# Turning the token-mixing weight with DMAs instead of TensorE

## The chip, the cores and the metric

The kernel runs on one core of one Trainium2 chip. The metric is the device time of one execution in microseconds (us); a run's time is given as the median of several executions. All inputs and the output lie in DRAM (HBM) at the start and the end. Everything else that is shown here comes from one profiled execution: the engines TensorE (PE, with its weight loads as PEld), VectorE (DVE), ScalarE (ACT), GpSimd (POOL) and SyncE (SP), and the DMA queues. Times "at 39.6" are microseconds from the start of that execution's span.

## The reference, cut to what matters

Two blocks follow one another. The first is a block-sorted attention: four batches, eight heads, 768 tokens, head dimension 64; eight blocks of 96 tokens are mixed by an 8 x 8 matrix that five Sinkhorn rounds have normalised, and attention runs inside each block. The second is an MLP with residual on the 768 x 512 activation of each batch:

```python
def _moe_ref(x, alpha1, beta1, w_tok, alpha2, beta2, w_ch1, w_ch2, lam):
    a1 = alpha1 * x + beta1
    tok = np.einsum('ts,bsd->btd', w_tok, a1)
    u = x + lam * tok
    a2 = alpha2 * u + beta2
    ch = np.maximum(a2 @ w_ch1, 0.0) @ w_ch2
    return (u + lam * ch).astype(np.float32)
```

`w_tok` is 768 x 768 and mixes tokens. TensorE contracts over the partitions of both its operands, so the sum over `s` needs `w_tok` with `s` on partitions, that is, its transpose. DRAM holds it with `t` on rows.

## The kernel before

The work is cut by batch `b` (0 to 3). Each engine gets its instructions in the order in which the program text issues them (the schedule is written out by hand, with no planner), and waits inside that order for the data it needs.

**Loads.** GpSimd's queue issues the loads that convert float32 to a 16-bit type on the way: `rawk`, `qn`, `raw0`/`rawv` for k, q and v, then (L143 to L145) six row tiles `wt16[n]`, each 128 rows of `w_tok` as 128 x 768 bf16, taken from the rotating tile name `hT`, which has ten buffers and is used for the hidden activations later. After `load_q(1)` and `load_k(1)` it issues `W1` (L735) and `W2` (L737). GpSimd also runs arithmetic in the same queue, so a DMA issue that waits holds up the arithmetic behind it. A GpSimd load waits until the load eight places before it on that queue has landed: the four `W2` issues at L737 wait for the two halves of `qn` and the two of `rawk` of batch 1. SyncE's queue issues the plain DMAs: vectors at the start, `a1lB`, `b1lB` and `lamB` (L718 to L720), then nothing until `v_relay(1)` (L412, L418), and the results later.

**The weight's turn.** `w_tok_block(ks, eng, pool)` (L288) turns one column block: six TensorE transposes, one for each row tile, into one PSUM bank, and one eviction by VectorE or ScalarE (`copy`, L147 to L151) to `w_tokT[:, ks, :]`. Six calls stand between the attention steps of batch 0 (L764 to L775), two evicted by VectorE and four by ScalarE. `w_tokT[p, ks, t]` is `w_tok[t, ks * 128 + p]`.

**Batch 0's way to the MLP.** `soft(0, p, g)` (L484) is two groups of small matmuls into a bank of the pool `psA`, which has two buffers, and one exponential on ScalarE (L502). `value(0, p)` (L522) is 24 matmuls into a `psA` bank (L516), a reciprocal (L528) and a product (L529) on VectorE, which writes its columns of `x16[0]`. The order at the end is `soft(0, 3, 0)`, `soft(0, 3, 1)`, and then `value` for p = 2, 1, 0, 3. `token_mix(0, 0)` (L583) needs all of `x16[0]`: six matmuls with `w_tokT` as the stationary operand (L589); then, only once, `row_sums` (L299, 36 matmuls at L303), which sums each row of `w_tok`; `row_part` (L575) makes of it the bias tile `rb[:, kt]`, on VectorE and ScalarE for the first two and on GpSimd (L579) for the other four. For each `kt` GpSimd adds `x + rb` (L597), VectorE adds the mixed part (L601, L602), ScalarE rounds the sum to bf16 (L603). `u_turn` (L614) turns it back for the hidden layer.

**The steady part.** `hidden` (L635) and `result` (L672) are the two dense layers; `weave` mixes the steps of the next batch's attention into them by fixed costs, so the order on each engine is fixed there too. The hidden activations take over the `hT` buffers: with six of the ten used by `wt16`, the fifth pair of the first `hidden` is the first to reuse one of those six. `w_tokT` serves all four batches.

Of the kernel before, what the change touches and what calls it, by code (L numbers as in the profile page):

```python
# [11 lines left out]
BF = mybir.dt.bfloat16  # L12
# [7 lines left out]
def kernel(  # L20
# [18 lines left out]
    B, H, S, D = q.shape  # L39
# [4 lines left out]
    NT = S // 128  # L44
# [12 lines left out]
    psM = ctx.enter_context(tc.tile_pool(name="psM", bufs=3, space=bass.MemoryType.PSUM))  # L57
# [4 lines left out]
    def wt(shape, dtype, name):  # L62
        return wts.tile(shape, dtype, name=name, tag=name)
# [4 lines left out]
    def tmp(shape, dtype, name, bufs):  # L68
        return work.tile(shape, dtype, name=name, tag=name, bufs=bufs)
# [4 lines left out]
    def bank(pool, dtype=FT):  # L74
        n = 512 if dtype is FT else 1024
        tag = "psM" if pool is psM else "psX"
        return pool.tile([128, n], dtype, name=tag, tag=tag)

    V, A, PE, G, SP = nc.vector, nc.scalar, nc.tensor, nc.gpsimd, nc.sync
# [23 lines left out]
    w_tokT = wt([128, NT, S], BF, "w_tokT")  # L103
# [39 lines left out]
    wt16 = [tmp([128, S], BF, "hT", 10) for _ in range(NT)]  # L143
# [3 lines left out]
    def copy(eng, dst, src):  # L147
        if eng is A:
            A.copy(dst, src)
        else:  # L150
            eng.tensor_copy(dst, src)  # L151

    def v_first_layout(part, quarter, eng):
        n = D // 16
        d0 = (part * 4 + quarter) * n
        dst = v0T[:, 0:BLK * D].rearrange("r (d t) -> r d t", t=BLK)
        src = raw0[0:64].rearrange("r (t d) -> r d t", d=D)
        copy(eng, dst[:, d0:d0 + n], src[:, d0:d0 + n])
# [22 lines left out]
    identbf = wt([128, 128], BF, "identbf")  # L181
# [88 lines left out]
    def big_p(b):  # L270
# [13 lines left out]
            pq[:].unsqueeze(1).to_broadcast([128, 2 * H, NB]),  # L284
            m16[:].unsqueeze(2).to_broadcast([128, 2 * H, NB]), ALU.mult,
        )

    def w_tok_block(ks, eng, pool):  # L288
        ps = bank(pool, BF)
        for tt in range(NT):  # L290
            PE.transpose(
                ps[:, tt * 128:(tt + 1) * 128], wt16[tt][:, ks * 128:(ks + 1) * 128], identbf[:]
            )
        copy(eng, w_tokT[:, ks, :], ps[:, 0:S])

    rowsum = wt([128, NT], FT, "rowsum")
    rb = wt([128, NT, C], FT, "rb")
# [27 lines left out]
    def q_pair(b, p, pool, eng):  # L325
        ps = bank(pool, F16)
        q_turn(b, p, ps)
        q_copy(b, p, ps, eng)
# [58 lines left out]
    def v_first(g, eng, pool):  # L387
        ps = bank(pool)
        for dd in range(8):
            d0 = (g * 8 + dd) * BLK  # L390
            m = 128 if dd < 7 else BLK
            PE.matmul(
                ps[0:m, dd * 64:(dd + 1) * 64], v0T[:, d0:d0 + m],
                PB[0][0:64, 0].rearrange("r l p i -> r l (p i)"), start=True, stop=True,
            )
        copy(
            eng, vS[0][:, :, g * 8:(g + 1) * 8],
            ps[0:BLK].rearrange("p (d c) -> p c d", c=64),
        )
# [84 lines left out]
    def soft(b, p, g):  # L484
        ps = bankA()
        for i in range(4):
            c = (g * 4 + i) * BLK
            for hl in range(2):
                r = slice(hl * 64, hl * 64 + 64)
                PE.matmul(  # L490
                    ps[:, hl, i * BLK:(i + 1) * BLK], kT[r, p * S + c:p * S + c + 128],
                    qT[b % 2][p][r, c:c + BLK], start=True, stop=False, skip_group_check=True,
                )
            for hl in range(2):
                r = slice(hl * 64, hl * 64 + 64)
                n = p * NB + g * 4 + i
                PE.matmul(  # L497
                    ps[:, hl, i * BLK:(i + 1) * BLK],
                    nmask[r, n:n + 1].to_broadcast([64, 128]), tp_of[p][r, :],
                    start=False, stop=True, skip_group_check=True,  # L500
                )
        A.activation(  # L502
            exps(b, p)[:, :, g * 4:(g + 1) * 4, 0:BLK],
            ps[0:BLK, :, 0:4 * BLK].rearrange("p l (i t) -> p l i t", t=BLK),
            AF.Exp, scale=scale,
        )
# [15 lines left out]
    def value(b, p):  # L522
        ps = bankA()
        for hl in range(2):
            products(b, p, hl, ps[:, hl])
        xg = ps[:, :, 0:NT * VP].rearrange("p l (s e) -> p l s e", e=VP)
        recip = tmp([128, 2, NT], FT, "recip", 2)
        V.reciprocal(recip[:], xg[:, :, :, D])  # L528
        V.tensor_tensor(  # L529
            x16[b % 2][:].rearrange("p s (l h d) -> p l s h d", l=2, d=D)[:, :, :, p],  # L530
            xg[:, :, :, 0:D],
            recip[:].unsqueeze(3).to_broadcast([128, 2, NT, D]), ALU.mult,
        )
# [184 lines left out]
    SP.dma_start(a1lB[:], vecs[0].partition_broadcast(128))  # L718
    SP.dma_start(b1lB[:], vecs[1].partition_broadcast(128))
    SP.dma_start(lamB[:], moe_lam.partition_broadcast(128))  # L720
    v_first_layout(0, 0, A)
    q_pair(0, 2, psM, A)
    v_first_layout(0, 1, A)
# [37 lines left out]
    soft(0, 1, 0)  # L761
    turn_first(3, 3)
    soft(0, 1, 1)
    w_tok_block(3, V, psM)  # L764
    v_first(6, V, psM)
    soft(0, 3, 0)
    soft(0, 3, 1)
    w_tok_block(0, V, psM)
    w_tok_block(5, A, psM)
    value(0, 2)  # L770
    w_tok_block(2, A, psM)
    value(0, 1)
    w_tok_block(1, A, psM)
    value(0, 0)
    w_tok_block(4, A, psM)  # L775
    value(0, 3)
    first = ahead(1)
    next(first)
# [18 lines left out]
    for b in range(B):  # L797
        n = b + 1
# [61 lines left out]
```

## Time and profile before

| | |
|---|---|
| time before, median of 3 | 297.47 us (297.2 to 297.64) |
| the profiled execution's own time | 297.77 us |
| its span, first to last instruction | 295.9 us |
| around the span | 1.87 us |
| mean granted TensorE clock | 0.983 |
| busy: PE, PEld, DVE, ACT, POOL | 278.2, 166.4, 170.2, 143.3, 71.9 us |
| chain that ended last, by engine | PE 75%, DVE 9%, POOL 5%, DMA 4%, ACT 4% |
| the turn of `w_tok`: PE L291, DVE L151, ACT L149 | 36 of 219 ns, 2 of 557 ns, 4 of 799 ns |
| DMA moved | 27.09 MB, mean 92 GB/s |

The span is the stretch in which the profiled core executed instructions; the time of that execution is longer by what lies before and after it. Busy times are sums over overlapping pipelined instructions, so a busy engine isn't necessarily the limit. The chain that ended last is followed back from the last instruction: at each step either to what released that instruction or to the one before it on its engine, so its shares say where a microsecond less would have been a microsecond less at the end, until another chain takes over. GB/s and KB count bytes at the destination of a DMA; a load that converts float32 to 16 bits reads twice as many.

### The profile page before, as it was taken

Reading aid. Unit: us, or ns where it says so; the run is one execution under the profiler, and the core shown is the slowest. Engines: PE = TensorE matmul, PEld = TensorE weight load, DVE = VectorE, ACT = ScalarE, POOL = GpSimd, SP = SyncE. Lnnn points to the kernel's source line nnn. Section 1 sums busy time; section 2 is a strip of 40 time slices with the busy share of each in tenths; the row PEclk is TensorE's granted clock in tenths of the full one; section 3 lists DMA queues with packets and bytes.
Section 4 is the critical chain, followed back from the end, with each engine's and each line's share of the span. In section 5 each row is a group of like instructions: output and inputs, shape, how many; then the busy total and the mean of one; then the engine's idle time right before and its main releaser. Section 6 shows DMA issues by size and latency. Waiting matters only on the chain.

```text
span 295.9 us, 7069 instructions
## 1 busy us (share of the span) xinstructions
PE 278.2 (94%) x3059; PEld 166.4 (56%) x3078; DVE 170.2 (58%) x315; ACT 143.3 (48%) x244; POOL 71.9 (24%) x86
## 2 busy tenths in 40 slices
PE   8968997799999999999999999999999999899994
PEld 6647854365556555565566455565566445545643
DVE  7887756885262669594452679592444684123224
ACT  3285857665436446664246455664344126811500
POOL 8399549910000532200000810000000900000000
PEclk9985999999999999999999999999999999999999
DMA  6997999999610039990110049100110010002012
GB/s 115 210 225 156 186 212 229 215 216 214 85 52 24 0 127 113 198 205 3 38 71 2 1 134 126 64 0 2 63 48 1 2 71 35 0 2 81 25 38 72
DMA packets 32135, 27.09 MB, mean 92 GB/s; under 512 B 19724, under 2 KB 26920, under 8 KB 32040
## 3 DMA queue, kind: packets, MB, share of 16 engines
q0 software_dynamic: 8976, 14.81, 28.4%
q1 hardware_dynamic: 23128, 11.82, 18.2%
q8 instruction: 24, 0.39, 0.5%
q14 instruction: 7, 0.06, 0.1%
HBM read 32.79 MB, written 8.65 MB: 140 GB/s over the span
## 4 chain that ended last, share of the span: by engine, by line
PE 75%; DVE 9%; POOL 5%; DMA 4%; ACT 4%; issue 1%; DVEq 0%; POOLq 0%
PE psM L635 28%; PE psM L672 23%; PE psM L589 7%; DMA u<-in_v_dram 4%; PE psA L516 3%; PE psA L490 2%; DVE kT L151 2%; PE psA L430 2%; PE psA L497 2%; DVE u L602 2%; POOL rb L579 2%; ACT a2T L625 2%; POOL u L597 2%; DVE x L529 1%; DVE mx L435 1%
## 5 line engine op out<-in xcount | busy, mean ns | idle before, releaser
L635 PE MATMUL psM<-a2T,W 128*128 128x384 bf16 x512 | 90.8, 326 | 0.9 <-ACT a2T L625 0.7
L672 PE MATMUL psM<-W,hT 128*128 128x512 bf16 x349 | 83.9, 379 | 1.6 <-issue 1.0
L645 ACT ACTIVATE hT<-psM 128x384 bf16<-128x384 f32 x96 | 46.5, 491 | 50.4 <-PE psM L635 49.1
L635 PEld LDWEIGHTS <-W 128*128 128x128 bf16 x512 | 47.8, 98 | 32.5 <-issue 2.3
L597 POOL TENSOR_TENSOR u<-x,rb 128x512 f32<-128x512 f16 x24 | 28.5, 1214 | 142.6 <-DVE x L529 140.7
L672 PEld LDWEIGHTS <-hT 128*128 128x128 bf16 x368 | 34.2, 98 | 37.2
L681 DVE TENSOR_TENSOR tmix<-psM,lamB 128x512 f32<-128x512 f32 x23 | 15.9, 690 | 39.4 <-PE psM L672 39.3
L643 DVE TENSOR_SCALAR hT<-psM 128x384 bf16<-128x384 f32 x32 | 17.7, 553 | 31.6 <-PE psM L635 27.2
L589 PE MATMUL psM<-x,w_tokT 128*128 128x512 f16 x144 | 34.7, 379 | 0.6 <-DVE x L529 0.6
L502 ACT ACTIVATE ET<-psA 96x768 f16<-96x768 f32 x28 | 21.1, 803 | 28.0 <-PE psA L497 28.0
L435 DVE TENSOR_REDUCE mx<-psA 96x8 f32<-96x768 f32 x30 | 27.3, 948 | 3.9 <-PE psA L430 3.7
L603 ACT CAST u<-u 128x512 bf16<-128x512 f32 x24 | 14.8, 618 | 21.9 <-DVE u L602 21.8
L602 DVE TENSOR_TENSOR u<-u,tmix 128x512 f32<-128x512 f32 x24 | 20.3, 846 | 6.5 <-POOL u L597 4.5
L589 PEld LDWEIGHTS <-w_tokT 128*128 128x128 bf16 x144 | 13.4, 98 | 15.3 <-DVE x L529 1.1
L601 DVE TENSOR_TENSOR tmix<-psM,a1lB 128x512 f32<-128x512 f32 x24 | 16.4, 683 | 3.1 <-PE psM L589 3.0
L625 ACT ACTIVATE a2T<-psM,cols 128x384 bf16<-128x384 bf16 x24 | 16.1, 670 | 3.4 <-PE psM L619 3.4
L682 DVE TENSOR_TENSOR u<-u,tmix 128x512 f32<-128x512 f32 x23 | 16.9, 734 | 1.5
L529 DVE TENSOR_TENSOR x<-psA,recip 128x768 f16<-128x768 f32 x16 | 15.3, 957 | 0.6
L490 PEld LDWEIGHTS <-kT 64*128 64x128 f16 x256 | 12.3, 98 | 5.2 <-issue 5.1
L490 PE MATMUL psA<-qT,kT 64*128 64x96 f16 x256 | 15.1, 212 | 0.2 <-ACT ET L502 0.2
L497 PE MATMUL psA<-tp,nmask 64*128 64x96 bf16 x256 | 15.0, 211 | 0.0
L528 DVE RECIPROCAL recip<-psA 128x12 f32<-128x12 f32 x16 | 3.7, 229 | 19.1 <-PE psA L516 19.1
(121 smaller groups left out, 295.1 us busy)
## 6 DMA issues: line engine op xcount, KB each, us to landing
out_dram<-u SPq DMA_DIRECT2D x23, 256.0 KB
W<-in_moe_w_ch_dram POOLq DMA_DIRECT2D x8, 512.0 KB, 20.2
rawk<-in_k_dram POOLq DMA_DIRECT2D x8, 384.0 KB, 7.6
qn<-in_q_dram POOLq DMA_DIRECT2D x8, 384.0 KB, 9.1
rawv<-in_v_dram POOLq DMA_DIRECT2D x6, 384.0 KB, 13.6
vscr<-rawv SPq DMA_DIRECT2D x3, 768.0 KB
vS<-vscr SPq DMA_DIRECT2D x8, 192.0 KB
hT<-in_moe_w_tok_dram POOLq DMA_DIRECT2D x6, 192.0 KB, 13.4
```

The costliest lines, as they stand in the source:

```text
L435: V.tensor_reduce(mx[b % 2][:, :, c:c + 4], ps[0:BLK, :, 0:4 * BLK].rearrange("p l (i t) -> p l i t", t=BLK), AXX, ALU.max,)
L490: PE.matmul(ps[:, hl, i * BLK:(i + 1) * BLK], kT[r, p * S + c:p * S + c + 128], qT[b % 2][p][r, c:c + BLK], start=True, stop=False, skip_g ...
L497: PE.matmul(ps[:, hl, i * BLK:(i + 1) * BLK], nmask[r, n:n + 1].to_broadcast([64, 128]), tp_of[p][r, :], start=False, stop=True, skip_grou ...
L502: A.activation(exps(b, p)[:, :, g * 4:(g + 1) * 4, 0:BLK], ps[0:BLK, :, 0:4 * BLK].rearrange("p l (i t) -> p l i t", t=BLK), AF.Exp, scale ...
L529: V.tensor_tensor(x16[b % 2][:].rearrange("p s (l h d) -> p l s h d", l=2, d=D)[:, :, :, p], xg[:, :, :, 0:D], recip[:].unsqueeze(3).to_br ...
L589: PE.matmul(ps[:], w_tokT[:, ks, kt * 128:(kt + 1) * 128], x[:, ks, :], start=(ks == 0), stop=(ks == NT - 1),)
L597: G.tensor_tensor(ub[:, kt], x[:, kt], rb[:, kt], ALU.add)
L602: V.tensor_tensor(ub[:, kt], ub[:, kt], t[:], ALU.add)
L625: A.activation(t[:], ps[:, 0:TOK], AF.Identity, bias=cols2[:, 1, ci:ci + 1], scale=cols2[:, 0, ci:ci + 1])
L635: PE.matmul(ps[:, 0:TOK], W1[:, ci, m * 128:(m + 1) * 128], a2T_of[b, half, ci][:], start=(ci == 0), stop=(ci == CT - 1),)
L645: A.activation(t, ps[:, 0:TOK], AF.Relu)
L672: PE.matmul(ps[:], hT_of[m][:, kk * 128:(kk + 1) * 128], W2[:, m, :], start=(m == 0), stop=(m == HT - 1),)
```

## The change

The function `w_tok_block` and its six calls go. Behind the issue of `lamB` SyncE issues six transposing DMAs, one for each row tile, from `wt16[n]` in SBUF to its place in `w_tokT`, all six column blocks at once: 128 x 768 in, 128 x 6 x 128 out. Each starts when its row tile has landed. `token_mix(0, kt)` reads the columns that the DMA of row tile `kt` wrote; `row_sums` reads all. Nothing else changes.

```diff
-    def w_tok_block(ks, eng, pool):
-        ps = bank(pool, BF)
-        for tt in range(NT):
-            PE.transpose(
-                ps[:, tt * 128:(tt + 1) * 128], wt16[tt][:, ks * 128:(ks + 1) * 128], identbf[:]
-            )
-        copy(eng, w_tokT[:, ks, :], ps[:, 0:S])
-
...
     SP.dma_start(lamB[:], moe_lam.partition_broadcast(128))
+    for n in range(NT):
+        SP.dma_start_transpose(w_tokT[:, :, n * 128:(n + 1) * 128], wt16[n][:])
     v_first_layout(0, 0, A)
...
     soft(0, 1, 1)
-    w_tok_block(3, V, psM)
     v_first(6, V, psM)
     soft(0, 3, 0)
     soft(0, 3, 1)
-    w_tok_block(0, V, psM)
-    w_tok_block(5, A, psM)
     value(0, 2)
-    w_tok_block(2, A, psM)
     value(0, 1)
-    w_tok_block(1, A, psM)
     value(0, 0)
-    w_tok_block(4, A, psM)
     value(0, 3)
```

## Prediction

> **What bounds the kernel now.** I read four views of the profile of before. The first is the chain of work that ended last, between 28 and 60 us, since the change lies in that stretch (start, length, what):
>
> ```profile
> 31.38 1.42 ACT ET L502 x2
> ...
> 33.36 0.78 PE psM L291 x12
> 34.13 0.76 PE psA L516 x24
> ...
> 34.91 0.24 DVE recip L528
> ...
> 38.62 0.97 DVE x L529
> ...
> 39.64 1.47 PE psM L589 x6
> 41.11 0.89 PE psM L303 x36
> ...
> 42.86 1.16 POOL u L597
> 44.02 2.08 POOL rb L579
> ```
>
> Of the 36 turns (L291) only twelve are on the chain, 0.78 us. Then four value steps follow at VectorE's pace, 34.91 to 39.59, and the other turns and their evictions lie beside them. From 42.86 to 52.6 GpSimd sets the pace (L597 and L579 in turn); from 58.8 on the chain is TensorE's dense layers to the end. So a gain ahead of 39.6 reaches the end if GpSimd and the DMAs let it.
>
> The second view is the order of time on ScalarE and GpSimd (start, length, what, idle time before and its releaser):
>
> ```profile
> 32.78 1.50 ACT L502 ACTIVATE u<-psA 96x768 f16<-96x768 f32 x2
> ...
> 36.98 0.74 POOL L737 DMA_DIRECT2D W<-in_moe_w_ch_dram  x1 [0.93 <-DMA rawk<-in_k_dram]
> 40.14 0.74 POOL L737 DMA_DIRECT2D W<-in_moe_w_ch_dram  x1 [2.42 <-DMA rawk<-in_k_dram]
> 42.86 1.16 POOL L597 TENSOR_TENSOR u<-x,rb 128x512 f32<-128x512 f16 x1 [1.98 <-DVE rb L579]
> ```
>
> GpSimd's last W2 issue waits for the second half of rawk to land, at 40.1, and ends at 40.88; its next instruction is the first link of GpSimd's stretch of the chain, 1.98 us later. This is the thinnest cover that the change touches.
>
> The third view is busy time by stage, of which the last three columns count: granted TensorE clock, DMA share, GB/s.
>
> ```profile
> 16.00:18.00 2.00, 0.86 (x28) 0.55 (x24) 1.56 (x3) 1.52 (x3) 1.68 (x3) 1.00 1.16 210
> 20.00:22.00 2.00, 0.95 (x16) 0.56 (x13) 0.97 (x3) 1.51 (x3) 2.00 (x4) 0.50 1.09 256
> 26.00:28.00 2.00, 2.00 (x48) 1.92 (x47) 1.48 (x4) 1.48 (x3) 1.94 (x3) 0.50 0.56 107
> 28.00:30.00 2.00, 2.00 (x47) 1.69 (x46) 1.31 (x4) 1.42 (x2) 2.00 (x4) 0.56 0.44 26
> 30.00:32.00 2.00, 2.00 (x59) 1.65 (x54) 1.87 (x7) 1.90 (x4) 2.00 (x5) 1.00 1.15 174
> 36.00:38.00 2.00, 2.00 (x55) 1.82 (x53) 1.93 (x5) 1.36 (x3) 0.79 (x2) 1.00 1.02 204
> ```
>
> The DMA engines are full at some 210 GB/s except for one pocket. At 107, 26 and 174 GB/s the rows from 26 to 32 moved 614 KB, where 210 would have moved 1260: 646 KB, or 3.1 us of full DMA work, is free there. The fourth view, of what one tile's instructions wait for, gives the landing of the row tiles: 12.1 to 13.8 us after their issues at 5.0 to 10.1, so the first lands near 18.4 and the last between 22.2 and 23.9.
>
> **What the change removes.** Behind the exponentials TensorE does twelve turns and then value(0, 2). Without them value(0, 2) waits for the next thing, its psA bank. The pool has two, and the free one is that of soft(0, 3, 0), whose exponential is the first of the two that begin at 32.78 with 1.50 us, so it ends at 33.53. Add the 0.06 us between the end of an exponential and TensorE's next start (32.78 to 32.84). The 24 matmuls take 0.91 from their first start (33.97 to 34.88 in the order of time on TensorE): 33.59 + 0.91 = 34.50, reciprocal at 34.53 in place of 34.91. **Gain 0.38 us**, not 0.78. After it VectorE is full (0.23 + 0.96 with a small overlap for each value), so nothing more comes.
>
> The other 24 turns and the evictions are worth nothing: ScalarE's four, 3.2 us, end ahead of a copy of rawv that waits 0.81 us for TensorE, and VectorE's second ends at 34.40, ahead of a reciprocal that waits for TensorE until 34.91. The first lies under ScalarE's exponentials, which set soft(0, 3, ·). Six banks of psM go unused; no step on the chain waits for one.
>
> **What it adds.** Six issues on SyncE, free from 18.64 (end of lamB's issue) until 45.24. An issue of vS, the SyncE issue with the most small runs, holds the queue for 1.35 us (median of ten): 8.1 us for six, over well ahead of 45.24, where v_relay(1) stands behind them. The added waits: TensorE's L589 at 39.26 for the first DMA, row_sums at 40.7 for the other five, and all of TensorE stands behind either; the fifth hidden pair, at about 62 us, for the first DMA's reading.
>
> How long the data take, no row shows; nothing here transposes in a DMA. They are 1.18 MB in 4608 runs of 256 bytes. From below: plain copies with long runs flow at 354 GB/s (50 to 51 us, where vscr<-rawv goes out of SBUF): 3.4 us. From above: runs of 128 bytes, alone on the DMA engines (vS, 112 to 117 us), flow at 92 GB/s: 12.8 us. If the number of runs counts, 256 bytes go at twice that: 6.4 us. Below nothing is excluded, as DMA work is added. The source lies in SBUF with rows of 1536 bytes as in the first row, the destination runs are nearer to the second; I take 4.5 us, between 3.4 and 6.4 and nearer to the first because its source is SBUF too; this is a choice. The Trainium skill, DMA: Bandwidth & Descriptors, section Latency and other measured facts, gives 261 GB/s for transposing DMAs with a non-contiguous middle dimension; the sum by it would also be 4.5 us. No run here shows it.
>
> The DMAs start between 18.6 and 24 beside full queues and end in the pocket, near 30, ten us ahead of need. Of 4.5 us, 3.1 fit into the pocket; 1.4 push the later loads back. What that meets: rawk's second half, and with it GpSimd's L597, has 1.98 - 0.38 = **1.6 us of cover**; W1 lands at the latest near 31.9 + 18.7 = 50.6 and is needed at 57.0; vS, last of the full stretch, has until value(1, 0) at 80.0, and the DMA share falls to 0.17 after 78. So 1.4 is just hidden, and the cover is thin: each microsecond of DMA work above 4.7 us costs a microsecond.
>
> **Sum.** -0.38 + 0 = -0.4 us. The profiled execution, 297.77 us (span 295.9 and 1.87 around it), goes to 297.4; it lay 0.30 above the median, so I apply the same difference to the median: 297.47 - 0.38 = **297.1 us**.
>
> **The rivals.**
>
> Loads pushed back (slower). The mechanism is that of the cover: the transposing DMAs delay rawk, the last W2 issue waits, GpSimd's L597 starts late and all behind it. It decides from 4.7 us of DMA work. At 6.4 us: 6.4 - 4.7 - 0.38 = +1.3, 298.8 us. At 12.8 us: +7.7, 305.2 us. For it speaks a DMA share of 1.0 or more before and after the pocket; against it, that the rate reached 256 GB/s at 20 to 22, so the queue isn't quite full there. 0.30, mostly with small prices.
>
> The chain's own figure (faster). If value(0, 2) could start at 33.36, all 0.78 us would go: 296.7 us. Against it stands the bank's reader. 0.12, with whatever else I overlook on that side.
>
> TensorE's clock. The rows show it at 0.50 from 20 to 28: between 16 and 19.5 TensorE was busy 1.84 us of 3.5 (53%, from the same view in half microseconds), then the clock halved, and came back at 29.7 after 3.4 us without a gap. After the change TensorE is busy from 33.3 to 39.3 for four values of 0.91 and 0.61 of v_group, 4.25 of 6.0 (71%), less than now. If that halves the clock for 3.4 us from 40, the 1.6 us of L589 and L303 that are still to come (they end at 42.0 - 0.4) double: +1.6 - 0.4 = +1.2, 298.7 us. Against it: 49 to 55 us, busy 2.8 of 6 (47%), kept 1.00. 0.06. The Trainium skill, TensorE: Matmul & The Clock Gate, section What's actually happening, describes a monitor with a free-running window of 3.4 us that halves the clock after an idle window. The trace agrees: 19.5 to 29.7 is three of them.
>
> One block at a time. If the 36 blocks of 128 x 128 pass singly, each at the 1.35 us of a vS issue, they take 48.7 us from 18.6 to 67.3, and row_sums waits from 40.7: +26.6 - 0.4 = +26, 324 us. Against it: one instruction covers six blocks, and vS issues, with twice the runs, pass in that time. 0.03. The Trainium skill's VectorE: DVE Perf Modes, section The three transpose paths, speaks against this change here: 1309 ns for one block by DMA, 390 by TensorE. The trace has 219 for TensorE; taken singly, the Trainium skill's figure would give an estimate of 47 us for all 36.
>
> **How the numbers follow.** Forecast 0.49; loads pushed back 0.30; the chain's figure 0.12; clock 0.06; singly 0.03. A measurement of this kernel can tell some 0.2% (0.6 us) from no change. Faster by more: 0.12 and 0.03 of the forecast's lower edge, 0.15. Within: 0.46 of the forecast and 0.03 of loads pushed back by little, 0.49. Slower: 0.27, 0.06 and 0.03, 0.36. The range goes from 296.4, under the chain's figure, to 300.5, which takes in the clock and up to 8.1 us of DMA work (8.1 - 4.7 - 0.38 = +3.0); some 0.14 is left out. The forecast's own range is 296.9 to 297.5.
>
> **What would show it.** Right: no L291; value(0, 2)'s reciprocal near 34.5; L589 near 39.3 with no DMA as its releaser; the last W2 issue before 41.7; GpSimd's first L597 near 42.5; the pocket at 26 to 30 filled. Wrong: L597 released by GpSimd's own late issue; L589 or L303 waiting for the transposing DMAs; a granted clock under 1.00 after 36; SyncE still busy with them past 35.

## The result, and the profile after

The changed kernel takes **317.47 us** (median of 4, 316.62 to 318.39) where the kernel before, on the same chip, takes 297.56: a ratio of 1.067 with an interval of 1.0638 to 1.0703, some 20 us slower. The prediction was 297.1 with a range of 296.4 to 300.5. The profiled execution took 317.55 us; its span is 315.6 us, 19.7 longer than before. In the code after the change the lines of the MLP have moved up by six or eight: L589 is now L581, L597 is L589, L579 is L571, L303 is L295, L516 is L508, L528 is L520, L529 is L521, L737 is L731.

The page of the profile after, the chain's shares by engine, and the hardware queue's line of the DMA part:

```profile
PE 65%; DMA 11%; DVE 10%; SPq 5%; POOL 4%; ACT 3%; issue 1%; DVEq 0%; POOLq 0%
...
q1 hardware_dynamic: 27928, 13.00, 22.1%
```

TensorE's share of the chain fell from 75% to 65% and DMA's rose from 4% to 11%. Before, q1 had 23,128 packets: the six transposing DMAs added 4,800, which are 4,608 runs of 256 bytes (288 on each of 16 DMA engines) and 192 small ones of 4 bytes, one of which marks the end of each DMA on each engine.

The chain that ended last, in the stretch that the prediction showed of before (start, length, what):

```profile
34.27 27.44 DMA w_tokT<-hT
61.75 0.32 PE psM L295 x6
...
62.96 1.14 POOL u L589
64.11 2.08 POOL rb L571
```

One line tells where the time went: 27.4 us for one transposing DMA, the last, and row_sums (L295), which reads all six, behind it. By the waits TensorE stood 11.1 us at row_sums for that one (15.2 with the one before). GpSimd's first L589 starts at 62.95, where before it started at 42.86: 20.1 us later. From there on the picture of before only moves: the dense layers' first step on the chain comes at 78.85 instead of 58.77, again 20.1. So all of the loss was made ahead of 63 us.

SyncE after, in order of time (start, length, what):

```profile
18.80 19.27 SPq L714 DMA_TRANSPOSE w_tokT<-hT  x6
```

GpSimd after, in order of time, with the idle time before and its releaser:

```profile
46.15 0.75 POOL L731 DMA_DIRECT2D W<-in_moe_w_ch_dram  x1 [4.51 <-DMA qn<-in_q_dram]
...
49.77 0.74 POOL L731 DMA_DIRECT2D W<-in_moe_w_ch_dram  x1 [1.27 <-DMA rawk<-in_k_dram]
62.95 1.16 POOL L589 TENSOR_TENSOR u<-x,rb 128x512 f32<-128x512 f16 x1 [12.44 <-PE psA L397]
```

SyncE is held from 18.8 to 38.1 by six issues. GpSimd's last W2 issue, 40.14 before, stands at 49.77, so the loads too are 9.6 us late; but GpSimd then idles 12.4 us for something later still. (The page names L397, TensorE's work right behind row_sums; what kept TensorE is the DMA in the chain.) Busy time by stage, the last columns being granted clock, DMA share and GB/s:

```profile
26.00:28.00 2.00, 2.00 (x49) 2.00 (x47) 1.61 (x4) 1.32 (x3) 1.94 (x3) 0.50 1.40 166
28.00:30.00 2.00, 2.00 (x51) 1.61 (x49) 1.15 (x4) 1.58 (x3) 2.00 (x4) 0.64 1.12 56
36.00:38.00 2.00, 0.85 (x17) 0.85 (x17) 0.57 (x2) 0.00 (x0) 0.00 (x0) 0.57 0.98 134
```

The pocket is filled, as forecast, by its share (1.40 and 1.12 instead of 0.56 and 0.44), but little moved in it: 56 GB/s from 28 to 30. From 36 to 38 TensorE works 0.85 of 2 us, and ScalarE and GpSimd not at all.

By the small packets that end each DMA, counted in the trace's own records, the six landed at 27.2, 32.3, 34.2, 38.6, 49.4 and 60.7 us on fifteen of the sixteen engines; one engine is later, and the sixth ends there at 61.4, just ahead of the 61.71 at which the wait on the chain ends. The first run of 256 bytes moved at 25.1. What happened while the last two were under way is in the packet counts of the two queues (packets, MB, share of 16 engines). The window from 52 to 54 us after the change:

```profile
q0 software_dynamic: 109, 0.40, 98.9%
q1 hardware_dynamic: 109, 0.03, 10.1%
```

109 load packets of W1, of some 4 KB, and 109 runs of 256 bytes: **the queues take turns, one packet each**, and each run of 256 bytes waits for a whole load packet. A turn takes 2.00 us x 16 engines / 109 = 0.29 us, of which the 256 bytes are 0.03. From 34.2 to 60.7 us each engine moved some 145 runs and 129 load packets, and the load packets took 24.7 of these 26.5 us. Earlier in the changed kernel it is not so: from 28 to 34 us 655 runs went beside only 56 load packets, so what slows both there isn't turns. The trace of the kernel before shows turns too, where vS (runs of 128 bytes, on SyncE) lies beside the loads of batch 2; its window from 66 to 68 us:

```profile
q0 software_dynamic: 481, 0.36, 116.3%
q1 hardware_dynamic: 479, 0.06, 41.2%
```

and 95 against 95 from 62 to 64 us. The prediction had this view at hand and didn't read it. The Trainium skill, DMA: Bandwidth & Descriptors, section Queues, rings and completion order, states the rule: each DMA engine goes round between the queues that have work, a packet at a time. The counts agree; its figure for a packet, some 9 to 17 descriptors, doesn't fit here, where a turn carried one run.

### The profile page after: what moved, and what is told of

The parts are those of the page before. It is cut to its first block, busy times and chain, and to the rows that moved or that the text cites. A ratio compares the mean times of both kernels' runs of the same rounds, so it can differ in the third digit from the quotient of the medians.

```text
span 315.6 us, 7022 instructions
## 1 busy us (share of the span) xinstructions
PE 283.5 (90%) x3042; PEld 167.3 (53%) x3042; DVE 169.5 (54%) x313; ACT 140.2 (44%) x240; POOL 71.8 (23%) x86
## 4 chain that ended last, share of the span: by engine, by line
PE 65%; DMA 11%; DVE 10%; SPq 5%; POOL 4%; ACT 3%; issue 1%; DVEq 0%; POOLq 0%
PE psM L627 26%; PE psM L664 21%; DMA w_tokT<-hT 9%; PE psM L581 5%; SPq L714 5%; PE psA L508 3%; DVE u L594 2%; DVE kT L151 2%; DMA vecs<-tmix 2%; PE psA L482 2%; PE psA L422 2%; POOL rb L571 2%; ACT a2T L617 2%; POOL u L589 1%; DVE tmix L593 1%; PE psA L489 1%
## 5 line engine op out<-in xcount | busy, mean ns | idle before, releaser
L664 PE MATMUL psM<-W,hT 128*128 128x512 bf16 x368 | 86.2, 379 | 0.0
L589 POOL TENSOR_TENSOR u<-x,rb 128x512 f32<-128x512 f16 x24 | 28.5, 1214 | 153.1 <-DVE x L521 140.6
L664 PEld LDWEIGHTS <-hT 128*128 128x128 bf16 x368 | 34.2, 98 | 37.2
L581 PE MATMUL psM<-x,w_tokT 128*128 128x512 f16 x144 | 37.3, 400 | 0.4 <-DVE x L521 0.4
L635 DVE TENSOR_SCALAR hT<-psM 128x384 bf16<-128x384 f32 x32 | 17.7, 553 | 31.3 <-PE psM L627 26.8
L494 ACT ACTIVATE ET<-psA 96x768 f16<-96x768 f32 x28 | 21.1, 803 | 28.0 <-PE psA L489 28.0
L595 ACT CAST u<-u 128x512 bf16<-128x512 f32 x24 | 14.8, 620 | 19.4 <-DVE u L594 19.3
L581 PEld LDWEIGHTS <-w_tokT 128*128 128x128 bf16 x144 | 14.0, 102 | 16.9 <-issue 3.9
L593 DVE TENSOR_TENSOR tmix<-psM,a1lB 128x512 f32<-128x512 f32 x24 | 16.4, 684 | 4.2 <-PE psM L581 4.1
L520 DVE RECIPROCAL recip<-psA 128x12 f32<-128x12 f32 x16 | 3.7, 231 | 24.0 <-PE psA L508 23.9
L508 PEld LDWEIGHTS <-ET 96*128 96x128 f16 x336 | 13.3, 102 | 5.2 <-issue 2.8
L521 DVE TENSOR_TENSOR x<-psA,recip 128x768 f16<-128x768 f32 x16 | 15.3, 957 | 0.6
L295 PE MATMUL psM<-ones_bf,w_tokT 128*128 128x1 bf16 x36 | 1.5, 167 | 15.2 <-DMA w_tokT<-hT 15.2
```

The source lines that it names most:

```text
L494: A.activation(exps(b, p)[:, :, g * 4:(g + 1) * 4, 0:BLK], ps[0:BLK, :, 0:4 * BLK].rearrange("p l (i t) -> p l i t", t=BLK), AF.Exp, scale ...
L508: PE.matmul(ps[:, s * VP:s * VP + D + 1], E[:, c0:c0 + 128], vS[b % 2][:, h * NB + i, 0:D + 1], start=(half == 0), stop=(half == 1), skip_ ...
L581: PE.matmul(ps[:], w_tokT[:, ks, kt * 128:(kt + 1) * 128], x[:, ks, :], start=(ks == 0), stop=(ks == NT - 1),)
L589: G.tensor_tensor(ub[:, kt], x[:, kt], rb[:, kt], ALU.add)
L593: V.tensor_tensor(t[:], ps[:], a1lB[:], ALU.mult)
L664: PE.matmul(ps[:], hT_of[m][:, kk * 128:(kk + 1) * 128], W2[:, m, :], start=(m == 0), stop=(m == HT - 1),)
```

## The experiments

The theory after this reading: the six DMAs aren't slow by themselves; their 288 runs an engine take turns with load packets of 0.08 to 0.47 us, and the loads in turn are pushed back. Rivals: the transposition itself is slow; the loads pushed back alone make the time; the transposing DMAs disturb more than turns explain.

**1. quiet.** The kernel before, and at its quiet end (the last batch's results) six transposing DMAs of the same size, from W1 into w_tokT, which nobody reads any more. They are extra work that leaves the output as it is.

```diff
         if n == B:
+            for m in range(NT):
+                SP.dma_start_transpose(
+                    w_tokT[:, :, m * 128:(m + 1) * 128],
+                    W1[:, m % CT, m // CT * S:(m // CT + 1) * S],
+                )
```

> The kernel before (its own 36 turns stay), with six transposing DMAs added late, at about 250 us, where the DMA engines are nearly idle: their source is W1 and they overwrite w_tokT after its last use, so nobody waits for them and only their own duration is seen. Theory of turns (a transposing packet of 256 bytes and a packet of GpSimd's loads alternate on each DMA engine, so a step costs what the load's packet costs): without loads the 288 steps take 4 to 5 us, at the rate of 26 to 28 us in the changed kernel (1085 packets in 2 us), and the time stays within 0.5 us of before. Rival, slow by themselves: (60.7 - 18.8) / 288 = 0.146 us a step, 42 us here too, from 250 to about 292.

Measured: 297.41 us, ratio 0.9997 (0.9966 to 1.0027). SyncE in order of time:

```profile
249.09 8.48 SPq L801 DMA_TRANSPOSE w_tokT<-W  x6
```

Six issues hold SyncE for 8.48 us, and their packets run from 250.4 to 258.6: 8.3 us for 1.18 MB, or 143 GB/s (one DMA takes 1.1 us, some 175 GB/s, with gaps of 0.2 to 0.3 us between them and one of 0.6). Not slow, in the sense of 27 us for one; but 8.3 us is more than the 4 to 5 expected of this run and the 4.5 of the prediction. 36 blocks in 8.3 us are 0.23 us a block.

**2. nowait.** Batch 0 reads the unturned row tiles in place of the turned ones, so nothing of batch 0 waits for the six DMAs, which run as in the changed kernel. The transposition of batch 0's weight is left out.

```diff
-                    rs[:, kt * 2:kt * 2 + 1], w_tokT[:, ks, kt * 128:(kt + 1) * 128],
+                    rs[:, kt * 2:kt * 2 + 1], wt16[ks][:, kt * 128:(kt + 1) * 128],
...
-                ps[:], w_tokT[:, ks, kt * 128:(kt + 1) * 128], x[:, ks, :],
+                ps[:], (wt16[ks] if b == 0 else w_tokT[:, ks])[:, kt * 128:(kt + 1) * 128], x[:, ks, :],
```

> The changed kernel, except that batch 0's mixing and row sums read the unturned row tiles wt16, which are there by 24 us, so that batch 0 waits for no transposing DMA; batches 1 to 3 read w_tokT as before. The weight of batch 0 is thereby not transposed. It tells the wait for w_tokT from the delay of GpSimd's loads. Theory of turns: the transposing DMAs land near 60 us as before; row_sums no longer wait; what is left is GpSimd's last W2 issue, which ended at 50.5 in the changed kernel against 40.9 before, so its first L589 starts at about 50.6 instead of 42.86: +7.7 us, about 305 us. Rival, the pushed-back loads make all of it: 317 us. Rival, the loads cost nothing: 297 to 300 us.

Measured: 311.26 us, ratio 1.0452 (1.0383 to 1.0522). GpSimd in order of time:

```profile
53.93 0.74 POOL L731 DMA_DIRECT2D W<-in_moe_w_ch_dram  x1 [2.92 <-DMA rawk<-in_k_dram]
54.69 1.17 POOL L589 TENSOR_TENSOR u<-x,rb 128x512 f32<-128x512 f16 x1
```

Without the wait at row_sums the time is still 13.5 us longer: the last W2 issue, which waits for rawk, comes 13.8 us late and L589 right behind it. So there are **two prices side by side**, the wait for the sixth DMA (+20 at L589) and the loads pushed back (+12), and in the changed kernel the first covers the second. It is more than the 305 us expected; 1.6 us of it is L571, which takes 2.08 us in all its four instances here, and in the kernel before only in the first (1.55 in the rest).

**3. plain.** The same 4,608 runs of 256 bytes as plain copies, without the transposition inside the blocks, which is left out.

```diff
-        SP.dma_start_transpose(w_tokT[:, :, n * 128:(n + 1) * 128], wt16[n][:])
+        SP.dma_start(
+            w_tokT[:, :, n * 128:(n + 1) * 128], wt16[n][:].rearrange("p (k t) -> p k t", t=128)
+        )
```

> The changed kernel with six plain copies in place of the transposing DMAs: the same source, the same destination, the same 4608 runs of 256 bytes, in the same place of SyncE's queue; the blocks arrive unturned, so the transposition is left out. Theory of turns in its narrow form (the transposition holds all sixteen engines in step, so that each step waits for the slowest engine's load packet): plain copies land well before 40 us, and the time is within 2 us of before. Rival, the number of runs: any 4608 packets alternate with the loads' packets, the copies land near 60 us and the time is 315 to 318 us.

Measured: 309.52 us, ratio 1.0394 (1.0315 to 1.0473). The waits:

```profile
PE psM L295 <- DMA w_tokT<-hT: 11.7, 1, 11.7
```

Plain copies take turns just the same (109 against 109 from 44 to 46 us) and the last lands at 52.7, so **most of the loss, 12 of 20 us, has nothing to do with transposing**. Neither expectation held: the copies land neither before 40 us nor near 60. The transposing DMAs cost 8 us more. Between 28 and 32 us of the changed kernel both queues nearly stand (16 and 21 load packets in the windows at 28 and 30; from 28 to 30 the middle one of rawv's 15 packets of 6 KB takes 2.0 us where 0.47 is usual; here 37 packets of the load queue and 856 of SyncE's move in that window), and its last W2 issue is 7.9 us later than here (49.77 against 41.88). This also shows the gain that was forecast: the first reciprocal comes at 34.38 and the first L581 at 39.10, 0.53 and 0.54 ahead of before. Of that, 0.20 is the exponentials' own: they begin at 32.58 instead of 32.78.

**4. w1_quarters.** W1 is loaded in four column quarters, so its packets are 1 KB instead of 4, and a turn beside W1 is shorter.

```diff
-    for ci in range(CT):
-        G.dma_start(W1[:, ci, :], moe_w_ch1[ci * 128:(ci + 1) * 128, :])
+    for c in range(4):
+        G.dma_start(
+            W1[:, :, c * 512:(c + 1) * 512],
+            moe_w_ch1.rearrange("(c p) h -> p c h", p=128)[:, :, c * 512:(c + 1) * 512],
+        )
```

> The changed kernel with W1 loaded by four DMAs of a quarter of its columns for all four row tiles, in place of four DMAs of one row tile: the same bytes in the same number of DMAs, with packets of 1 KB at the destination instead of 4 KB. Theory of turns: in the stretch of the W1 packets (from 42 us on, 0.29 us for a pair of packets on one engine) a step falls to the time of a 1 KB packet, about 0.1 us; some 75 steps are left at 42 us, so the last transposing DMA lands near 42 + 75 x 0.1 = 50 instead of 60.7, and the time falls by about 10 us, to 306 to 309 us. Rival, the two queues share the engines by time or by bytes: nothing changes, 317 us.

Measured: 311.83 us, ratio 1.0472 (1.0404 to 1.0539): 5.6 us less than the changed kernel. From 52 to 54 us:

```profile
q0 software_dynamic: 317, 0.31, 91.0%
q1 hardware_dynamic: 319, 0.08, 30.3%
```

Three times as many runs pass in the same time, since the packets that they wait for are a quarter as long. The direction is that of the turns; the rival, a share by time or by bytes, said no change. The size is less than the 306 to 309 us expected. Two reasons are likely but not shown one by one: W1 itself moves more slowly (0.31 MB in these 2 us instead of 0.40), and half the runs had their turns beside qn and rawk.

**5. hold.** GpSimd copies one column of each of the six turned tiles ahead of `load_q(1)`, so the large loads can't start before the six DMAs have landed.

```diff
+    seen = wt([128, NT], BF, "seen")
+    G.tensor_copy(seen[:], w_tokT[:, 0, 0:S:128])
     load_q(1)
     load_k(1)
```

> The changed kernel with one small copy on GpSimd ahead of load_q(1): it reads a column of every row tile's place in w_tokT, so GpSimd issues the loads of batch 1, W1 and W2 only when all six transposing DMAs have landed. Theory of turns: with no load packets to alternate with (only what is left of rawv), the DMAs run at the pace that they have alone (8.3 us for six, 250.4 to 258.6 in the quiet run) and land by 31 to 35 us; row_sums waits for nothing; the loads start at 31 to 35 instead of 27.7, so the last W2 issue comes 4 to 7 us after that of before (40.1) and GpSimd's first L589 2.5 to 5.5 us after 42.86: 300 to 303 us. Rival, the transposition itself is what is slow in this place, whatever the loads do: landing near 60 us and 317 us or more.

Measured: 303.14 us, ratio 1.0171 (1.0117 to 1.0225). The copy runs at 36.1, behind a wait of 8.3 us:

```profile
36.10 0.19 POOL L727 COPY seen<-w_tokT 128x6 bf16<-128x6 bf16 x1 [8.28 <-DMA w_tokT<-hT]
```

With the two kept apart, except for what is left of rawv, the sixth DMA lands at 35.5 instead of 60.7. What is left is the loads' late start, +5.1 at L589.

**6. early.** The six go ahead of the three broadcast loads on SyncE, so they begin at 21 us instead of 25.

```diff
+    for n in range(NT):
+        SP.dma_start_transpose(w_tokT[:, :, n * 128:(n + 1) * 128], wt16[n][:])
     SP.dma_start(a1lB[:], vecs[0].partition_broadcast(128))
     SP.dma_start(b1lB[:], vecs[1].partition_broadcast(128))
     SP.dma_start(lamB[:], moe_lam.partition_broadcast(128))
-    for n in range(NT):
-        SP.dma_start_transpose(w_tokT[:, :, n * 128:(n + 1) * 128], wt16[n][:])
```

> The changed kernel with the six transposing DMAs issued ahead of a1lB, b1lB and lamB on SyncE instead of behind them. In the changed kernel the first transposing packet moved only at 25.1 us, behind those three on SyncE's queue, though its row tile had landed near 18.4. Theory of turns: between 18.4 and 26.5 GpSimd's queue has few packets left (about 480 on 16 engines, 30 for each), so most of the 288 steps go by without a turn and the six land by 28 to 31 us, before the loads of batch 1 take their turns; the last W2 issue stays near 40, the forecast's 0.38 us is gained, and the time is 297.0 to 298.0 us. Rival, the place on the queue does not matter, since the DMAs of row tiles 4 and 5 cannot start before 24 us anyway: they meet the loads, landing is past 45 us and the time over 305 us.

Measured: 302.54 us, ratio 1.0146 (1.0118 to 1.0174). My expectation was missed. The sixth lands at 33.8 and nobody waits for it, but:

```profile
45.70 0.74 POOL L731 DMA_DIRECT2D W<-in_moe_w_ch_dram  x1 [1.18 <-DMA rawk<-in_k_dram]
46.46 1.18 POOL L589 TENSOR_TENSOR u<-x,rb 128x512 f32<-128x512 f16 x1
```

That is, link by link, the prediction's rival "loads pushed back": rawk lands late, the last W2 issue is at 45.7 instead of 40.1, and L589 starts 3.6 us late right behind it. L571 at 2.08 us in all four instances adds 1.6.

**7. early_rawv.** early, with the second half of rawv also issued some 6 us sooner, to empty the load queue ahead of qn.

```diff
+    load_v(1, (1,))
     for quarter in range(4, 16):
-        if quarter == 12:
-            load_v(1, (1,))
         v_first_layout(0, quarter, G)
```

> As early, and GpSimd issues the second half of rawv directly behind its two memsets, at about 16 us, instead of at 22.7: its 64 packets of 6 KB were still on the way at 28 to 34 us in the changed kernel and held up both queues there (235 transposing packets in 4 us). Theory of turns: they now pass before the transposing DMAs' last two row tiles, which land by 28 to 30 us, at least 1 us before those of early; the time is that of early or up to 0.5 us less. Rival, these packets do no harm: landing and time as in early.

Measured: 312.91 us, ratio 1.0481 (1.0438 to 1.0524): missed, and in the wrong direction. The earlier rawv takes the DMA time in which the first tiles moved in early; the sixth tile then lands at 52.4 and b1lB, behind it on SyncE, at 57.4:

```profile
33.08 24.36 DMA b1lB<-vecs
```

It is steep: the sixth tile's first run moved near 30.4 us in early, and the tile was through at 33.8; here it moved near 36.0, and the tile was through at 52.4.

**8 to 10. W2's issues later.** If GpSimd's wait for rawk is all that is left in early, W2's issues can go behind the MLP's first batch, where they wait for nothing. Tried in early (early_w2late), in the kernel before (before_w2late, the control) and in the changed kernel (after_w2late).

```diff
-    for m4 in range(4):
-        G.dma_start(
-            W2[:, m4 * 4:(m4 + 1) * 4, :],
-            moe_w_ch2[m4 * 512:(m4 + 1) * 512, :].rearrange("(m p) c -> p m c", p=128),
-        )
...
+    for m4 in range(4):
+        G.dma_start(
+            W2[:, m4 * 4:(m4 + 1) * 4, :],
+            moe_w_ch2[m4 * 512:(m4 + 1) * 512, :].rearrange("(m p) c -> p m c", p=128),
+        )
     load_k(2)
     load_q(2)
     load_v(2)
```

> As early (transposing DMAs ahead of a1lB, b1lB and lamB), and GpSimd's four W2 issues moved from behind W1 to just ahead of load_k(2), behind the token mixing of batch 0. In early the DMAs landed by 34 us and row_sums waited for none, but rawk came 5.6 us late and the last W2 issue, which waits for it, held GpSimd's first L589 until 46.46 (42.86 before), 3.6 us of the 4.9. Theory (the cover of GpSimd's queue is what is lost in early): L589 starts near 42.8, rawk is still in time for its matmuls at 48.5, and the time is that of before_w2late within 0.6 us. Rival, the later rawk, qn and W1 themselves are waited for by TensorE: 1 to 4 us above before_w2late.

> The kernel before with GpSimd's four W2 issues moved to just ahead of load_k(2), as a control for early_w2late: no transposing DMAs, TensorE does its turns. W2 then lands about 12 to 15 us after 56 and is needed at 72.6; vS and the loads of batch 2 share the DMA engines with it. Expected within 0.5 us of before, 297 to 298.5 us; if the crowding at 56 to 76 us costs something, up to 2 us more, which early_w2late then has as well.

> The changed kernel with GpSimd's four W2 issues moved to just ahead of load_k(2); the transposing DMAs stay behind a1lB, b1lB and lamB. Theory of turns, as a count: at 34.2 us, 144 of the 288 steps are left, and the loads that are queued give each engine 64 packets of qn, 8 of rawk and 32 of W1, so 104 turns instead of the 144 of the changed kernel, of which 40 fell to W2; after them the queue is empty and the other 40 steps run free. These 104 packets are 3.67 MB, 18 us at 205 GB/s, and the 144 steps of 31 ns add 4.5: landing near 57 instead of 60.7, 313 to 314 us. Rival, the loads that GpSimd's own issue delays make the time: without the W2 issues on the way to L589 it falls to 300 to 304 us.

Measured: early_w2late 302.23 us, ratio 1.0143 (1.0103 to 1.0184); before_w2late 297.85, 0.9994 (0.9971 to 1.0017); after_w2late 315.66, 1.0593 (1.0537 to 1.0649). Moving W2 costs nothing by itself, and in the changed kernel it gains little (313 to 314 us was expected; the rival's 300 to 304 is out), since there the sixth DMA sets the end. In early_w2late the loss didn't go away; it moved. Its chain:

```profile
31.17 16.36 DMA b1lB<-vecs
47.57 0.05 issue
47.62 0.50 DVE rb L571
48.16 0.10 issue
48.26 1.16 POOL u L589
```

GpSimd no longer waits for rawk. But the sixth tile is through at 38.6 here, against 33.8 in early, and b1lB, a broadcast load in packets of 2 KB behind the six on SyncE, now takes the turns: 16.4 us from its issue to its landing, and VectorE's L571, which ran at 42.1 in early, waits for it. Why the sixth is later isn't shown; the two kernels differ only in W2's issues, the first of which came at 35.85 in early.

**11. early_w2late_g.** The same, with the three broadcast loads issued by GpSimd ahead of `load_q(1)`, in the load queue itself.

```diff
-    SP.dma_start(a1lB[:], vecs[0].partition_broadcast(128))
-    SP.dma_start(b1lB[:], vecs[1].partition_broadcast(128))
-    SP.dma_start(lamB[:], moe_lam.partition_broadcast(128))
...
+    G.dma_start(a1lB[:], vecs[0].partition_broadcast(128))
+    G.dma_start(b1lB[:], vecs[1].partition_broadcast(128))
+    G.dma_start(lamB[:], moe_lam.partition_broadcast(128))
     load_q(1)
```

> The six transposing DMAs lead on SyncE, W2's issues stand late as in the run before, and the three small broadcast loads that stood behind the six on SyncE (in that run the second of them landed 16.4 us after its issue, at 47.5, and L571 waited for it) are issued by GpSimd, on the queue of the large loads, just ahead of load_q(1). Theory: all of the change's cost is small packets of one queue taking turns with the load packets of the other, on whatever transfer comes to lie there; with the broadcasts in the load queue itself, in order, and the six under way from 21 us, little is left to take turns: the sixth row tile lands by 39, L589 starts within 1.2 us of before's 42.86 (GpSimd's three more issues cost 1.5 us of its own time), and the time is 297.3 to 299.0 us. Rival: the six slow the other queue while they run (load packets of 2 to 3 us in 28 to 34 us), so qn, rawk and rawv still come late by 3 us or more and the time is 300.5 us or more, with a wait for one of them ahead of L589.

Measured: 303.19 us, ratio 1.0183 (1.0159 to 1.0207). Both expectations fell: the time is the rival's, and yet nothing is late ahead of L589. GpSimd:

```profile
42.43 1.16 POOL L589 TENSOR_TENSOR u<-x,rb 128x512 f32<-128x512 f16 x1 [4.88 <-DVE rb L571]
```

That is 0.43 us **earlier** than before, and the first L581 starts at 39.22 instead of 39.64: here the change's gain is real, and in the right size. The loss comes 35 us later, in the waits from 55 to 130 us:

```profile
PE psA L508 <- DMA vS<-vscr: 4.1, 1, 4.1
```

W1's packets end at 56.5 here and at 49.0 in before_w2late. So vS, batch 1's relayed values in runs of 128 bytes on SyncE, no longer finds an idle gap. In before_w2late vS runs alone (1,511 of its packets from 54 to 56 us, and no load packet) and ends at 59.0; here it meets W2 from 58 on, and from 66 to 68 us

```profile
q0 software_dynamic: 374, 0.37, 109.0%
...
q1 hardware_dynamic: 374, 0.05, 30.4%
```

it goes in turns with it, ending at 83.4. TensorE waits for it, 4.1 of the 5.2 us. It is the same mechanism, turns, with another victim. That the six DMAs alone made W1 late is not shown: the edit itself puts the three broadcast loads, 192 packets of 4 KB or 0.79 MB, into the load queue ahead of W1, at 210 GB/s an estimated 3.7 of these 7.5 us.

**12. early_half.** If the price is the DMA work that finds no idle DMA time, half of it should cost nothing: the first three row tiles are turned by DMAs at the early place, the last three by TensorE as before.

```diff
-        for tt in range(NT):
+        for tt in range(3, NT):
             PE.transpose(
                 ps[:, tt * 128:(tt + 1) * 128], wt16[tt][:, ks * 128:(ks + 1) * 128], identbf[:]
             )
-        copy(eng, w_tokT[:, ks, :], ps[:, 0:S])
+        copy(eng, w_tokT[:, ks, 384:S], ps[:, 384:S])
...
+    for n in range(3):
+        SP.dma_start_transpose(w_tokT[:, :, n * 128:(n + 1) * 128], wt16[n][:])
     SP.dma_start(a1lB[:], vecs[0].partition_broadcast(128))
```

> Half the change, at the early place: the first three row tiles of w_tok are turned by DMAs ahead of the three broadcast loads on SyncE, the last three by TensorE as before (18 turns and the right halves of the six evictions stay). Theory: what the change costs at this place is the DMA work that finds no idle DMA time (8.3 us for six alone, 3.1 us of idle time) and the turns that whatever lies behind it takes. Three row tiles are 4.15 us of work, and in the kernels with this order the third landed at 29 us, where qn's packets begin; about 1 us is over, so the last issue of W2 stands at 40.1 to 41.6 (before 40.14), L597's place on GpSimd starts no more than 0.7 us later than before's 42.86, and the time is 297.2 to 298.8 us. Rival: the price goes with the number of transposing DMAs wherever they lie, half of the 4.9 us of six at this place: 300.0 us (299.4 to 300.8).

Measured: 297.51 us (12 executions), ratio 1.0000 (0.9979 to 1.0021). GpSimd:

```profile
40.80 0.74 POOL L739 DMA_DIRECT2D W<-in_moe_w_ch_dram  x1 [1.18 <-DMA rawk<-in_k_dram]
42.62 1.17 POOL L597 TENSOR_TENSOR u<-x,rb 128x512 f32<-128x512 f16 x1 [1.09 <-DVE rb L579]
```

The three land by 29.2, just where qn's packets begin. The last W2 issue is 0.7 us late, which the 1.98 us of cover takes, and the stretch on GpSimd begins 0.24 us early. Half the transposing DMAs cost nothing where six at the same place cost 4.4 us (by early's ratio): a step and not a slope, as the theory has it and the rival has not. No version that was tried beats the kernel before.

## Why the prediction was wrong, point by point

- **The step that failed** is "the DMAs start between 18.6 and 24 beside full queues and end in the pocket, near 30, ten us ahead of need". It priced them as bytes at a rate, filling what others left free. Already the start was late: the first run moved at 25.1 us, behind the packets of the three broadcast loads on the same queue, where early, with the six ahead of them, has it at 21.1. In place of the overlap the runs showed turns: beside a busy load queue a run of 256 bytes moves only once a load packet has, so the time is a number of runs (288 an engine) times what the packets on the other queue last (0.08 us for qn, 0.32 for W1, 0.47 for rawk). By 34.2 us half the runs were through; the other 144 took 26.5 us. The counts of before, 95 against 95 beside vS, would have shown the turns. Turns are not all: three tiles by 34.2, where 8.3 us alone bring six, come of the start at 25.1 and of the stretch from 28 to 34 us in which both queues slow; the cause of that stretch stays open.
- **The size of the work**, 4.5 us chosen between 3.4 and 12.8, measured 8.3 alone (quiet); nearest was the term by the number of runs, 6.4. By the prediction's own rule (each microsecond above 4.7 costs one) 8.3 gives 8.3 - 4.7 - 0.4 = +3.2. That is near early's +3.6 at L589, and far from the +20 of the change: the mis-sized term isn't the larger part, the turns are.
- **The gain of 0.38 us** was right in cause and nearly in size. Without the turns TensorE waits, as told, for the exponential (0.28 to 0.38 us, released by L494), and from the start of the two exponentials to the first reciprocal it takes 1.80 us in plain, early, early_w2late and early_w2late_g, where before it took 2.13: a gain of 0.33. What the first reciprocal gains in all (0.53 in plain, 0.41 in early_w2late_g, 0.06 in early) differs by when the exponentials begin, 32.58 to 33.05 against 32.78. In the changed kernel the gain can't be seen, since TensorE stands 2.7 us ahead of the last matmul of the first value step.
- **SyncE's 8.1 us**: 8.48 alone, so right as an issue cost, but 19.3 beside the loads. It cost nothing, as v_relay(1) came later still.
- **The cover of 1.6 us** was real and thin, as told. early and nowait went through it by the path named; early_half stayed inside it.
- **Loads pushed back**, the rival, was right in mechanism, and its price of 1.3 to 7.7 takes in early (+4.4). In the changed kernel it is there (W2's last issue +9.6) but covered by the wait at row_sums. The prediction weighed the delay that the six cause to the loads, never the delay that the loads cause to the six.
- **One block at a time** gave 324, nearest to the result, by a mechanism that quiet refutes: 0.23 us a block, not 1.35. Its place was right, though: row_sums, waiting for the sixth.
- **The chain's own 0.78** was not seen; 0.54 is the most in any run. **TensorE's clock** did fall to 0.50, from 36.3 to 67.0 us, a stretch in which TensorE mostly waits (0.85 us busy of 2 from 36 to 38, 0.32 from 50 to 52); from 62.95 on the steps of the chain have before's lengths, so little is to be put down to it.

What stays open: why transposing DMAs and loads slow each other beyond turns (8 us between plain and the change). Being in flight together isn't enough: in early, from 28 to 30 us, 1,166 packets of SyncE's queue and 48 of the load queue, 32 of them rawv's, moved in the window in which the changed kernel moved 81 and 16. Open too is why L571 takes 2.08 us in all four instances in nowait, hold and early, and only in the first in the others; these three are the runs in which the first L589 follows a W2 issue without a gap, and no run tells whether that is the cause.

## What to carry to other kernels

Here a DMA of short runs on one queue beside a load on another couldn't be priced by its bytes. In such a case, count its runs for each DMA engine, multiply by the length of the packets that it will lie beside, and look in the trace for a place where two queues already overlap, whose packet counts show the turns. Before moving work from a compute engine to DMAs, find the DMA time that is idle in that stage; what fitted in cost nothing here (early_half), and what didn't was paid by whichever small transfer came to lie beside the loads. When a fix only moves the loss, look for the new victim of the same mechanism before looking for another cause.

## What the runs showed of the hardware

- In the windows shown from 44 us on, two queues with work alternate one for one, whether the run is transposed (109 and 109), plain (109 and 109) or a relayed load (374 and 374), beside load packets of 4 KB or 1 KB and less. From 28 to 34 us of the changed kernel they don't.
- In the changed kernel, transposing DMAs and load packets in flight together both nearly stop for a while: 56 GB/s from 28 to 30 us, with the middle one of rawv's packets at 2.0 us instead of 0.47. In early, in the same window, they don't.
- In the same stretch a fetch of TensorE's instructions, one 16 KB packet on the instruction queue, came at 34.7 instead of 28.9, and TensorE stood idle with nothing named as the cause:

```profile
37.15 0.21 PE L508 MATMUL psA<-vS,x 96*128 96x65 f16 x1 [2.70 <-issue]
```

That the fetch is the cause is inferred from the times: in nowait, w1_quarters, after_w2late and hold, too, TensorE goes on 2.3 to 2.7 us after that packet's start (34.65, 34.85, 34.69 and 32.71 us); in plain and early, where it came at 30.7 and 31.3, the wait is absent. It cost nothing here, as the later wait covers it.
